# Zeros ahead of the first products, a broadcast in float32r halves, and a clamp on GpSimd: one change to an attention and two-MLP kernel

## The chip, the core and the metric

The kernel runs on one core of a Trainium2 chip. The metric is the device time of one execution in microseconds (us), the median over the runs of a kernel. A core has five engines that run side by side, each through its own instructions in order: TensorE (PE in the profile, with its weight loads as PEld), VectorE (DVE), ScalarE (ACT), GpSimd (POOL) and SyncE (SP), which here issues all DMA transfers. They wait for each other through semaphores.

## What is computed

Two batches of eight heads, 576 positions, head size 64: causal attention with a bias from a running sum, then an MLP with a leaky ReLU, then a second MLP with four experts that are weighted by probabilities.

```
scores = q @ k^T / 8
cum    = cumsum(max(s, 0))                      # per head, along the sequence
scores = where(causal mask, -1e9, scores + min(-(cum_i - cum_j), 0))
x      = softmax(scores) @ v                    # heads side by side: 1152 x 512
x      = leaky(x @ w_in) @ w_out                # 512 -> 2048 -> 512, float64 inputs
p      = probs / (sum(probs) + 1e-9)
out    = sum over e of p[:, e] * (relu(x @ w1[e]) @ w2[e])   # 4 experts, 512 -> 1024 -> 512
```

`moe_w_in` and `moe_w_out` come as float64; the kernel sees them as pairs of 32-bit words.

## The kernel before, in words

Everything of the MLPs is multiplied as float32r in two halves (a high part and the remainder): `products` (L150) issues three matmuls for each pair, high by high, low by high, high by low. The attention is plain float32, which TensorE runs in two passes for each product.

**Attention.** The 1152 rows are cut into four parts, each for four pairs of heads; one part and one pair make a `Unit` (L319). For each of its tiles of 128 queries and each head of the pair it runs four steps, which trail each other by a few tiles: `scores` (L329) masks the diagonal block of `nck` on GpSimd (L339), multiplies q by k (L342, tile `ps_sc`), lets VectorE combine the product with `nck` and take the row minimum (L343, tile `z`), and ScalarE take the exponential (L347); `transposes` (L349, tile `ps_pt`) turns z for the product with v, `values` (L359, tile `ps_o`) multiplies and scales by the row sums (L367, L368, L371), and `finish` (L373, tile `ps_x`) turns the result into the halves of x (L387, L388).

**The running sum.** `cumulative` (L274) loads s for all 16 heads, 16 partitions of 576, and scans it on VectorE (L281, tile `cum`). `nck` is its row for each of two heads, spread over all 128 partitions. For the first unit `load_pair` does this by a float32 product of a column of the identity with `cum` (L308, tile `ps_nck`) and a copy by ScalarE (L309); for all others cum goes to DRAM (L282) and comes back by a DMA with a stride of zero (L312).

**Weights.** `load_w` brings pieces of 128x1024. A piece of w_in or w_out is converted from float64 once (`convert`, L73, 16 pieces in all): two loads fill `r64` (a pool of two buffers, in which `pos` and `cum` also lie), ScalarE scales the upper words (L84), VectorE clamps (L85), shifts (L86), and joins the lower word and the sign (L87, L88). The result goes to DRAM (L97) for the later phases. Every piece is then split: ScalarE rounds it to the high half (L104), GpSimd subtracts (L105).

**Order.** The program is written as generators that are woven together (`weave`, L413): attention of the first part, then the first MLP on 512 rows beside the attention of the next, and so on. The order in which instructions finally stand on each engine is set by the framework's scheduler at build time, which has its own cost estimates, so that an edit in one place moves instructions in others. `ps_sc` and the pool of `ps_pt`, `ps_x` and `ps_nck` have two PSUM buffers each.

The quoted lines are the clamp and what stands around it, as printed in the functions below.

Of the kernel before, what the change touches and what calls it, by code (L numbers as in the profile page):

```python
# [8 lines left out]
F32 = mybir.dt.float32  # L9
# [3 lines left out]
ALU = mybir.AluOpType  # L13
# [5 lines left out]
def attention_moe_moe2(ctx: ExitStack, tc: tile.TileContext, q, k, v, s, w_in, w_out, probs, w1, w2, out):  # L19
# [31 lines left out]
    def f32(ap):  # L51
        return ap.bitcast(F32)
# [20 lines left out]
    def convert(src, raw, rows):  # L73

        r64 = r64p.tile([P, 1024, 2], U32, tag="r64", name="r64")
        for i in range(2):
            a, c = slice(i * rows // 2, (i + 1) * rows // 2), slice(i * 512, (i + 1) * 512)  # L80
            nc.sync.dma_start(r64[:, c].rearrange("p (a b) t -> p a (b t)", a=rows // 2), src[:, a])
        lower, upper = r64[:, :, 0], r64[:, :, 1]
        bits = raw.bitcast(U32)
        nc.scalar.activation(raw, upper.bitcast(F32), AF.Abs, scale=65536.0)  # L84
        nc.vector.tensor_scalar(raw, raw, 2.0, LARGEST, ALU.max, ALU.min)  # L85
        nc.vector.tensor_scalar(bits, bits, 3, None, ALU.logical_shift_left)  # L86
        nc.vector.scalar_tensor_tensor(bits, lower, 29, bits, ALU.logical_shift_right, ALU.bitwise_or)  # L87
        nc.vector.scalar_tensor_tensor(bits, upper, 0x80000000, bits, ALU.bitwise_and, ALU.bitwise_or)  # L88
# [205 lines left out]
    def load_pair(n, b, hp, i0, i1):  # L294


        q0, q1 = tiles[i0][0], tiles[i1 - 1][2]
        rows, h = slice(hp * P, (hp + 1) * P), b * H + 2 * hp
        kr = ap.tile([P, S], F32, tag="kr", name="kr")
        nc.sync.dma_start(kr[:, :q1], k[b].rearrange("h d s -> (h d) s")[rows, :q1])  # L300
        qz, vs = q_pads[n % 2], v_s[n % 4]
        for j in range(2):
            nc.sync.dma_start(qz[j * D : (j + 1) * D, j, : q1 - q0], q[b, 2 * hp + j, :, q0:q1])
        nck = ap.tile([P, 2, S], F32, tag="nck", name="nck")
        if n == 0:
            for j in range(2):
                ps = ps_t.tile([P, 512], F32, tag="pt", name="ps_nck")[:, :q1]
                nc.tensor.matmul(ps, ident[:BH, h + j : h + j + 1].to_broadcast([BH, P]), cum[:, :q1], start=True, stop=True)  # L308
                nc.scalar.copy(nck[:, j, :q1], ps)  # L309
        else:  # L310
            src = cum_d[h : h + 2, 0:q1]
            nc.sync.dma_start(nck[:, :, :q1], bass.AP(tensor=src.tensor, offset=src.offset, ap=[[0, P], [S, 2], [1, q1]]))  # L312
        full = min(q1 // P, QT - 1)
        nc.sync.dma_start(vs[:, :full].rearrange("p t h c -> p t (h c)"), v[b, : full * P, rows].rearrange("(t p) c -> p t c", p=P))
        if i1 == QT:
            nc.sync.dma_start(vs[P - S % P :, QT - 1].rearrange("p h c -> p (h c)"), v[b, full * P :, rows])
        return kr, qz, nck, vs
# [178 lines left out]
```

## Time and profile before

| | |
|---|---|
| median of 3 runs | 768.6 us (768.29 to 769.13) |
| the profiled execution: its own time | 767.84 us |
| its span, first to last instruction | 766.1 us |
| TensorE busy | 746.2 us, 97% of the span |
| VectorE, ScalarE, GpSimd busy | 317.7, 287.9, 229.6 us |
| moved by DMA | 79.56 MB |

All rows shown here come from that one execution. Times in them count from the span's start. A row of the timeline gives the start, the length, the engine, the line in the kernel, the operation, what is written from what, and in brackets how long the engine had been idle before and what ended that. TensorE's products overlap their neighbours, so their lengths add up to more than the time that they take together. Names of tiles appear without their buffer numbers (`raw`, `z`), and a DMA's issue on SP is not its landing.

### The profile page before, as it was taken

Reading aid. Unit: us, or ns where it says so; the run is one execution under the profiler, and the core shown is the slowest. Engines: PE = TensorE matmul, PEld = TensorE weight load, DVE = VectorE, ACT = ScalarE, POOL = GpSimd, SP = SyncE. Lnnn points to the kernel's source line nnn. Section 1 sums busy time; section 2 is a strip of 40 time slices with the busy share of each in tenths; the row PEclk is TensorE's granted clock in tenths of the full one; section 3 lists DMA queues with packets and bytes.
Section 4 is the critical chain, followed back from the end, with each engine's and each line's share of the span. In section 5 each row is a group of like instructions: output and inputs, shape, how many; then the busy total and the mean of one; then the engine's idle time right before and its main releaser. Section 6 shows DMA issues by size and latency. Waiting matters only on the chain.

```text
span 766.1 us, 10681 instructions
## 1 busy us (share of the span) xinstructions
PE 746.2 (97%) x4124; PEld 648.6 (85%) x4124; DVE 317.7 (41%) x663; ACT 287.9 (38%) x587; POOL 229.6 (30%) x174
## 2 busy tenths in 40 slices
PE   7798999999999999999999999999999999999997
PEld 4576788778889999999898888988989889888886
DVE  3998685974544443323322222222222222222222
ACT  3766665564565564654320221211303112032010
POOL 3551143453344244676311220312203121122100
PEclk9899999999999999999999999999999999999999
DMA  8778945764243222435210110202001101000002
GB/s 254 245 229 279 316 147 178 258 210 151 66 142 115 79 83 83 154 129 163 78 56 28 56 54 1 83 28 56 29 28 56 56 30 53 28 28 0 1 28 96
DMA packets 44931, 79.56 MB, mean 104 GB/s; under 512 B 4528, under 2 KB 23472, under 8 KB 44880
## 3 DMA queue, kind: packets, MB, share of 16 engines
q1 hardware_dynamic: 44880, 78.88, 31.5%
q8 instruction: 32, 0.52, 0.3%
q14 instruction: 19, 0.16, 0.1%
HBM read 68.08 MB, written 10.78 MB: 103 GB/s over the span
## 4 chain that ended last, share of the span: by engine, by line
PE 87%; DVE 5%; DMA 5%; issue 1%; POOL 0%; ACT 0%; SPq 0%; POOLq 0%; DVEq 0%; ACTq 0%
PE ps_d L154 39%; PE ps_u L154 37%; PE ps_sc L342 5%; PE ps_o L365 4%; PE ps_pt L356 2%; DMA r<-in_moe_w_in_dram 1%; DMA kr<-in_k_dram 1%; DVE z L343 1%; DVE raw L87 1%; DMA r<-in_moe_w_out_dram 1%; DMA pn<-in_moe_domain_probs_dram 1%; DMA nck<-cum_d 1%; DVE raw L88 1%; DVE st L367 0%; DVE raw L86 0%
## 5 line engine op out<-in xcount | busy, mean ns | idle before, releaser
L105 POOL TENSOR_TENSOR w<-raw,w 128x1024 fp32r<-128x1024 f32 x80 | 193.9, 2434 | 376.4 <-ACT w L104 374.9
L154 PE MATMUL ps_u<-y,w 128*128 128x320 f32 (+1 forms) x1152 | 201.5, 336 | 0.7 <-DVE yacc L207 0.7
L154 PEld LDWEIGHTS ps_u<-y,w 128*128 128x128 f32 x1152 | 185.1, 188 | 17.0 <-ACT w L104 0.9
L154 PE MATMUL ps_d<-w,ht 128*128 128x512 f32 x864 | 197.3, 389 | 0.0
L154 PEld LDWEIGHTS ps_d<-w,ht 128*128 128x128 f32 x864 | 161.8, 188 | 33.2
L104 ACT CAST w<-raw 128x1024 fp32r<-128x1024 f32 x80 | 83.1, 1044 | 170.7 <-issue 163.1
L154 PE MATMUL ps_u<-x,w 128*128 128x320 f32 (+1 forms) x576 | 116.7, 349 | 1.5 <-DVE ht L188 1.0
L154 PE MATMUL ps_d<-ht,w 128*128 128x320 f32 (+1 forms) x576 | 116.9, 349 | 0.0
L191 DVE SCALAR_TENSOR_TENSOR ht<-ps_u,ht 128x320 fp32r<-128x320 f32 (+1 forms) x96 | 53.6, 558 | 146.9 <-ACT ht L190 146.9
L154 PEld LDWEIGHTS ps_u<-x,w 128*128 128x128 f32 x576 | 92.0, 189 | 11.3 <-issue 2.3
L190 ACT ACTIVATE ht<-ps_u 128x320 fp32r<-128x320 f32 (+1 forms) x96 | 47.1, 491 | 142.0 <-PE ps_u L154 142.0
L154 PEld LDWEIGHTS ps_d<-ht,w 128*128 128x128 f32 x576 | 91.4, 188 | 8.7 <-issue 1.3
L228 DVE SCALAR_TENSOR_TENSOR oacc<-ps_d,pn,oacc 128x512 f32<-128x512 f32 x63 | 47.3, 751 | 122.8 <-PE ps_d L154 122.8
L342 PE MATMUL ps_sc<-kr,qz 128*128 128x448 f32 (+4 forms) x192 | 68.7, 455 | 4.5 <-DVE mn L343 4.3
L339 POOL TENSOR_SCALAR_AFFINE_SELECT nck<-nck 128x128 f32<-128x128 f32 x80 | 33.2, 428 | 120.7 <-DVE mn L343 60.0
L365 PEld LDWEIGHTS ps_o<-vs,pv 128*128 128x128 f32 x480 | 63.1, 196 | 6.0 <-DVE xo L371 1.9
L365 PE MATMUL ps_o<-vs,pv 128*128 128x64 f32 x480 | 64.0, 271 | 1.3 <-DVE xo L371 1.0
L347 ACT ACTIVATE z<-z,mn 128x512 f32<-128x512 f32 (+4 forms) x80 | 48.4, 606 | 44.2 <-DVE mn L343 43.8
L343 DVE CUSTOM_DVE_ANT_0 z<-ps_sc,nck 128x512 f32<-128x512 f32 (+4 forms) x80 | 40.7, 511 | 32.9 <-PE ps_sc L342 23.6
L357 ACT COPY pv<-ps_pt 128x512 f32<-128x512 f32 (+3 forms) x96 | 39.1, 422 | 25.1 <-PE ps_pt L356 22.9
L342 PEld LDWEIGHTS ps_sc<-kr,qz 128*128 128x128 f32 x192 | 32.9, 197 | 15.7 <-DVE mn L343 7.2
L356 PE MATMUL ps_pt<-ident,z 128*128 128x128 f32 x240 | 42.1, 279 | 3.5 <-ACT pv L357 2.4
(43 smaller groups left out, 354.1 us busy)
## 6 DMA issues: line engine op xcount, KB each, us to landing
raw<-w_f SPq DMA_DIRECT2D x32, 512.0 KB, 3.2
raw<-in_moe_w_dram SPq DMA_DIRECT2D x32, 512.0 KB, 3.4
r<-in_moe_w_in_dram SPq DMA_DIRECT2D x16, 512.0 KB, 6.5
w_f<-raw SPq DMA_DIRECT2D x16, 512.0 KB, 3.3
r<-in_moe_w_out_dram SPq DMA_DIRECT2D x16, 512.0 KB, 5.6
nck<-cum_d SPq DMA_DIRECT2D x8, 576.0 KB, 5.9
vs<-in_v_dram SPq DMA_DIRECT2D x12, 256.0 KB, 4.6
kr<-in_k_dram SPq DMA_DIRECT2D x8, 288.0 KB, 4.9
```

The source lines that it names most:

```text
L104: nc.scalar.copy(w[:, 0], raw)
L105: nc.gpsimd.tensor_tensor(w[:, 1], raw, f32(w[:, 0]), ALU.subtract)
L154: nc.tensor.matmul(ps, a, b, start=(i == 0), stop=(i == len(pairs) - 1))
L190: nc.scalar.activation(hi, ps, AF.Relu)
L191: nc.vector.scalar_tensor_tensor(lo, ps, 0.0, f32(hi), ALU.max, ALU.subtract)
L228: nc.vector.scalar_tensor_tensor(oacc[tt], ps, p, oacc[tt], ALU.mult, ALU.add)
L342: nc.tensor.matmul(ps, self.qz[:, j, own], self.kr[:, keys], start=True, stop=True)
L343: nc.vector.tensor_tensor_reduce(out=z[:, keys], in0=ps, in1=nck[:, j, keys], scale=-(D ** -0.5), scalar=3.0e38 if pc == 0 else mn[:, 0:1] ...
L347: nc.scalar.activation(z, z, AF.Exp, bias=mn[:, pc : pc + 1], scale=-1.0, accum_out=self.st[i][:, j : j + 1])
L356: nc.tensor.transpose(pt[:, (kt - k0) * P : (kt - k0 + 1) * P], z[:, tiles[kt][0] : tiles[kt][2]], ident)
L357: nc.scalar.copy(pv[:, k0:k1].rearrange("p t q -> p (t q)"), pt)
L365: nc.tensor.matmul(o[:, j], pv[:, kt], self.vs[:, kt, j], start=(kt == 0), stop=(kt == i))
```

## The change

Three edits. First, 8 products of a 128x128 tile of zeros by itself are issued on TensorE at the start, into a PSUM tile that nothing reads. Second, the first unit's `nck` is no longer a float32 product: the first 512 columns of `cum` are split into a high half (ScalarE) and a remainder (VectorE) in a new tile `cum0`, the two columns of the identity are copied as float32r (`pick`), and each head's row is two accumulated float32r products. `cum0` is a third allocation in the pool of two `r64` buffers. Third, the clamp in `convert` runs on GpSimd instead of VectorE. Below the edits, line numbers grow by up to 12.

```diff
@@ convert
         nc.scalar.activation(raw, upper.bitcast(F32), AF.Abs, scale=65536.0)
-        nc.vector.tensor_scalar(raw, raw, 2.0, LARGEST, ALU.max, ALU.min)
+        nc.gpsimd.tensor_scalar(raw, raw, 2.0, LARGEST, ALU.max, ALU.min)
         nc.vector.tensor_scalar(bits, bits, 3, None, ALU.logical_shift_left)
@@ cumulative
-    cum = None
+    cum0 = None
+    pick = const.tile([BH, 2], F32R, name="pick")
...
+        idle = ap.tile([P, P], F32, tag="idle", name="idle", bufs=1)
+        nc.vector.memset(idle, 0.0)
+        nothing = ps_t.tile([P, 512], F32, tag="pt", name="nothing")
+        for _ in range(8):
+            nc.tensor.matmul(nothing[:, :P], idle, idle, start=True, stop=True)
         pos, cum = (r64p.tile([P, 2048], F32, tag="r64", name=n)[:BH] for n in ("pos", "cum"))
+        nc.scalar.copy(pick, ident[:BH, :2])
...
         nc.vector.tensor_tensor_scan(cum, spos, zero, 0.0, ALU.add, ALU.add)
+        cum0 = r64p.tile([P, 2048], F32R, tag="r64", name="cum0")[:BH, : 2 * sizes[0]].rearrange("p (l k) -> p l k", l=2)
+        nc.scalar.copy(cum0[:, 0], cum[:, : sizes[0]])
+        nc.vector.tensor_tensor(cum0[:, 1], cum[:, : sizes[0]], f32(cum0[:, 0]), ALU.subtract)
         nc.sync.dma_start(cum_d, cum)
@@ load_pair, first unit
-                nc.tensor.matmul(ps, ident[:BH, h + j : h + j + 1].to_broadcast([BH, P]), cum[:, :q1], start=True, stop=True)
+                for l in range(2):
+                    nc.tensor.matmul(ps, pick[:, j : j + 1].to_broadcast([BH, P]), cum0[:, l, :q1], start=(l == 0), stop=(l == 1))
```

The scheduler gives the whole early part another order. Three places, with the program's instructions as they stand on an engine.

TensorE from its first instruction on, before (`ps_nck` is the broadcast, `ps_sc` the scores, `ps_pt` the transposes):

```order
0 L491 UNCONDITIONAL_BRANCH
1 L308 MATMUL ps_nck<-cum,ident 128x512 x2
2 L342 MATMUL ps_sc<-kr,qz 128x512 x2
3 L342 MATMUL ps_sc<-kr,qz 128x384
4 L356 MATMUL ps_pt<-ident,z 128x128 x4
```

and with the change:

```order
0 L503 UNCONDITIONAL_BRANCH
1 L282 MATMUL nothing<-idle 128x128 x8
2 L354 MATMUL ps_sc<-kr,qz 128x512
3 L320 MATMUL ps_nck<-cum_135,pick 128x512
4 L354 MATMUL ps_sc<-kr,qz 128x512
5 L320 MATMUL ps_nck<-cum_135,pick 128x512 x3
6 L354 MATMUL ps_sc<-kr,qz 128x384 x2
```

The zeros stand first, and the first scores ahead of the broadcast, which is now four products of one pass.

GpSimd behind its first memsets, before (L339 is the mask, L105 the subtraction for the split weights):

```order
12 L339 AFFINE_SELECT nck<-nck 128x128 x13
13 L105 TENSOR_TENSOR w<-raw,w 128x1024
14 L339 AFFINE_SELECT nck<-nck 128x128 x4
15 L105 TENSOR_TENSOR w<-raw,w 128x1024
16 L339 AFFINE_SELECT nck<-nck 128x128 x4
```

and with the change:

```order
12 L351 AFFINE_SELECT nck<-nck 128x128 x10
13 L85 TENSOR_SCALAR raw<-raw 128x1024
14 L351 AFFINE_SELECT nck<-nck 128x128
15 L85 TENSOR_SCALAR raw<-raw 128x1024
16 L351 AFFINE_SELECT nck<-nck 128x128 x4
17 L105 TENSOR_TENSOR w<-raw,w 128x1024
18 L351 AFFINE_SELECT nck<-nck 128x128 x3
19 L105 TENSOR_TENSOR w<-raw,w 128x1024
20 L85 TENSOR_SCALAR raw<-raw 128x1024
21 L351 AFFINE_SELECT nck<-nck 128x128 x2
```

The clamps stand between masks, the first two of them ahead of the first subtraction. Among the first masks, five of the first unit now stand ahead of the second unit's; before it was two.

VectorE where the second piece of weights is converted, before (z operations are L343, those named mn end them; `pn` and `prow` are the probabilities):

```order
41 L343 ISA z,mn<-ps_sc,nck 128x384
42 L343 ISA mn 128x1
43 L66 RECIPROCAL prow<-prow 128x9
44 L368 RECIPROCAL st<-st 128x2
45 L87 SCALAR_TENSOR_TENSOR raw<-r_556,raw 128x1024
46 L371 TENSOR_TENSOR xo<-ps_o,st 128x128
47 L67 TENSOR_TENSOR pn<-pn,prow 128x36
48 L367 TENSOR_SCALAR st<-st 128x2
49 L88 SCALAR_TENSOR_TENSOR raw<-r_556,raw 128x1024
50 L368 RECIPROCAL st<-st 128x2
51 L343 ISA z,mn<-ps_sc,nck 128x384
```

and with the change, from the probabilities on (L355 is L343, r_564 the first piece; L379 and L380 are L367 and L368, L383 is L371):

```order
37 L67 TENSOR_TENSOR pn<-pn,prow 128x36
38 L355 ISA z,mn<-ps_sc,nck 128x512
39 L355 ISA mn 128x1
40 L86 TENSOR_SCALAR raw<-raw 128x1024
41 L355 ISA z,mn<-ps_sc,nck 128x384
42 L355 ISA mn 128x1
43 L87 SCALAR_TENSOR_TENSOR raw<-r_564,raw 128x1024
44 L383 TENSOR_TENSOR xo<-ps_o,st 128x128
45 L379 TENSOR_SCALAR st<-st 128x2
46 L88 SCALAR_TENSOR_TENSOR raw<-r_564,raw 128x1024
47 L380 RECIPROCAL st<-st 128x2
48 L383 TENSOR_TENSOR xo<-ps_o,st 128x128
```

L67 now stands ahead of the whole first conversion, and z operations stand between the steps of a conversion; the clamp is gone from this queue. On SP the load of the second unit's `nck` stands behind three loads of v instead of ahead of them.

## Rows read from the trace of the kernel before

**Rows 1.** The page: busy us of each engine with its share of the span and its instructions, and the chain that ended last, by engine.

```profile
PE 746.2 (97%) x4124; PEld 648.6 (85%) x4124; DVE 317.7 (41%) x663; ACT 287.9 (38%) x587; POOL 229.6 (30%) x174
...
PE 87%; DVE 5%; DMA 5%; issue 1%; POOL 0%; ACT 0%; SPq 0%; POOLq 0%; DVEq 0%; ACTq 0%
```

**Rows 2.** Three stretches: us, then busy us and instructions of PE, PEld, DVE, ACT and POOL, the granted clock as a share of full speed, DMA's busy share and GB/s.

```profile
20.00:40.00 20.00, 16.62 (x86) 12.43 (x87) 18.37 (x49) 13.10 (x35) 9.76 (x10) 0.85 0.78 247
40.00:60.00 20.00, 18.80 (x114) 14.56 (x113) 18.53 (x43) 13.73 (x34) 10.04 (x10) 0.97 0.74 239
...
160.00:766.00 606.00, 601.48 (x3345) 535.58 (x3343) 196.47 (x382) 190.96 (x366) 167.86 (x93) 1.00 0.21 68
```

**Rows 3.** Waits of TensorE from 13 to 140 us: who waited for whom, us in total, times, the longest.

```profile
PE ps_sc L342 <- DVE mn L343: 4.3, 7, 2.2
PE ps_pt L356 <- ACT pv L357: 2.4, 4, 1.2
PE ps_o L365 <- DVE xo L371: 1.0, 2, 0.8
```

**Rows 4.** The timeline from 0 to 15 us, some rows of it, by engine.

```profile
1.66 1.19 SPq L303 DMA_DIRECT2D qz<-in_q_dram  x2
...
7.08 1.57 SPq L314 DMA_DIRECT2D vs<-in_v_dram  x3
...
3.01 1.35 DVE L281 TENSOR_TENSOR_SCAN cum<-pos 16x576 f32<-16x576 f32 x1
...
10.42 0.69 DVE L343 CUSTOM_DVE_ANT_0 z<-ps_sc,nck 128x512 f32<-128x512 f32 x1 [6.06 <-PE ps_sc L342]
...
13.39 0.56 DVE L343 CUSTOM_DVE_ANT_0 z<-ps_sc,nck 128x384 f32<-128x384 f32 x1 [0.58 <-POOL nck L339]
...
7.23 0.29 POOL L339 TENSOR_SCALAR_AFFINE_SELECT nck<-nck 128x128 f32<-128x128 f32 x1 [3.06 <-ACT nck L309]
...
12.51 1.03 POOL L339 TENSOR_SCALAR_AFFINE_SELECT nck<-nck 128x128 f32<-128x128 f32 x4 [3.27 <-DMA nck<-cum_d]
...
4.50 3.75 PE L308 MATMUL ps_nck<-cum,ident 16*128 16x512 f32 x4 [4.50 <-DVE cum L281]
8.18 5.06 PE L342 MATMUL ps_sc<-kr,qz 128*128 128x512 f32 x6
13.03 0.94 PE L356 MATMUL ps_pt<-ident,z 128*128 128x128 f32 x4
...
14.46 0.60 PE L356 MATMUL ps_pt<-ident,z 128*128 128x128 f32 x4
```

**Rows 5.** Groups by line and shape on ScalarE and VectorE from 0 to 180 us: count, busy us, mean ns of one, idle time before them.

```profile
L387 ACT CAST x<-ps_x 128x512 fp32r<-128x512 f32 x4 | 2.3, 568 | 0.0
...
L388 DVE TENSOR_TENSOR x<-ps_x,x 128x512 fp32r<-128x512 f32 x4 | 2.7, 679 | 0.0
```

**Rows 6.** DMA issues from 0 to 14 us: KB of one, median us from issue to landing.

```profile
qz<-in_q_dram SPq DMA_DIRECT2D x4, 128.0 KB, 3.2
```

**Rows 7.** Groups by line and shape on VectorE from 0 to 180 us, columns as in rows 5; and the line on the instructions of L367 over the whole span, with the shortest, median and longest in ns.

```profile
L87 DVE SCALAR_TENSOR_TENSOR raw<-r,raw 128x1024 uint32<-128x1024 uint32 x16 | 23.3, 1454 | 0.1
L88 DVE SCALAR_TENSOR_TENSOR raw<-r,raw 128x1024 uint32<-128x1024 uint32 x16 | 21.0, 1310 | 0.0
L367 DVE TENSOR_SCALAR st<-st 128x2 f32<-128x2 f32 x28 | 16.0, 572 | 3.4 <-ACT z L347 3.3
L86 DVE TENSOR_SCALAR raw<-raw 128x1024 uint32<-128x1024 uint32 x16 | 12.8, 798 | 0.1
L85 DVE TENSOR_SCALAR raw<-raw 128x1024 f32<-128x1024 f32 x16 | 11.0, 688 | 13.9 <-ACT raw L84 13.9
...
L367 DVE TENSOR_SCALAR st<-st x35: 142/170/2371, 13.9 to 245.5; 128x2 f32<-128x2 f32 x35
...
  ACT raw L84: 13.9, 10
```

(The last line is of L85's instructions: until what their engine sat idle before them, us and times.)

**Rows 8.** Groups by line and shape on GpSimd from 0 to 180 us, columns as in rows 5.

```profile
L105 POOL TENSOR_TENSOR w<-raw,w 128x1024 fp32r<-128x1024 f32 x15 | 37.7, 2518 | 17.1 <-ACT w L104 17.1
L339 POOL TENSOR_SCALAR_AFFINE_SELECT nck<-nck 128x128 f32<-128x128 f32 x58 | 26.9, 479 | 86.3 <-DMA nck<-cum_d 40.4 <-DVE mn L343 39.5 <-ACT nck L309 4.5
L290 POOL MEMSET qz<- 64x512 f32 x4 | 2.1, 519 | 0.1
L292 POOL MEMSET vs<- 64x128 f32 x4 | 0.6, 196 | 0.0
```

**Rows 9.** The timeline from 27 to 47 us, some rows of it, by engine; and the stretch from 0 to 80 us for the instructions of L85 alone, columns as in rows 2.

```profile
27.52 3.32 POOL L105 TENSOR_TENSOR w<-raw,w 128x1024 fp32r<-128x1024 f32 x1
...
28.75 2.14 DVE L67 TENSOR_TENSOR pn<-pn,prow 128x36 f32<-128x36 f32 x1
...
31.02 1.21 DVE L88 SCALAR_TENSOR_TENSOR raw<-r,raw 128x1024 uint32<-128x1024 uint32 x1
...
44.97 2.47 DVE L86 TENSOR_SCALAR raw<-raw 128x1024 uint32<-128x1024 uint32 x1
...
32.82 0.92 PE L342 MATMUL ps_sc<-kr,qz 128*128 128x256 f32 x4 [2.23 <-DVE mn L343]
...
0.00:80.00 80.00, 5.49 (x8) 0.96 0.81 254
```

**Rows 10.** The stretch from 34 to 42 us, columns as in rows 2; the last but two is the granted clock.

```profile
34.00:42.00 8.00, 8.00 (x34) 6.59 (x33) 6.83 (x16) 5.07 (x14) 2.06 (x2) 0.57 0.82 250
```

More of the change, by code (lines that the diff above doesn't have):

```diff
@@ L271, in attention_moe_moe2 @@
     cum_d = dram.tile([BH, S], F32, name="cum_d")
-    cum = None
+    cum0 = None
+    pick = const.tile([BH, 2], F32R, name="pick")
     def cumulative():
-        nonlocal cum
+        nonlocal cum0
+        idle = ap.tile([P, P], F32, tag="idle", name="idle", bufs=1)
[3 more added lines that the diff above has]
+            nc.tensor.matmul(nothing[:, :P], idle, idle, start=True, stop=True)
         pos, cum = (r64p.tile([P, 2048], F32, tag="r64", name=n)[:BH] for n in ("pos", "cum"))
+        nc.scalar.copy(pick, ident[:BH, :2])
         spos, zero, cum = pos[:, :S], pos[:, S : 2 * S], cum[:, :S]
```

## The prediction

> **What bounds the kernel now.** I read the page's busy shares and chain first [rows 1]. TensorE is busy 97% of the span and holds 87% of the chain that ended last, so the run ends when its products are done: only its idle time, its time at the low clock, or products that disappear can move the end. The stages say where such time lies [rows 2]: of 606 us behind 160, TensorE misses 4.5; from 20 to 60 it misses 4.6 of 40, and there VectorE is busy 18.4 and 18.5 of every 20. All three edits act ahead of 160 us. TensorE's longest waits between 13 and 140 us [rows 3]: 4.3 + 1.0 us end with VectorE, 2.4 with an eviction by ScalarE. So VectorE is the engine to relieve, early. The execution read here took 767.84 us for a span of 766.1; the median of the runs is 768.6, 0.76 higher. A measurement of this kernel tells about 0.2% (1.5 us) from no change.
>
> **Zeros and the first broadcast.** The first products start at 4.50, when the scan (3.01 + 1.35) is done [rows 4]. Four passes of ps_nck hold TensorE until 8.18; then come the scores, and on VectorE the first z starts at 10.42 and the third at 13.39. The clock is low all this while: four transposes take 0.94 us at 13.03 but 0.60 at 14.46, and a pass of 512 columns some 0.85 us (3.7 by 4) where it should take half.
>
> Added: one memset on VectorE, which waits there for the scan's input, and 8 products of 128 columns in two passes each. At the low clock a pass of that size takes some 0.21 us (0.94 less the last one's tail, by four), so 16 take 3.4 us, from about 1.2 to 4.6. TensorE had no work then, so they cost nothing. Added behind the scan: a cast on ScalarE and a subtraction on VectorE of 512 columns, 0.57 and 0.68 by the x rows of the same width [rows 5]; the low half is there at 4.36 + 0.6 + 0.7 + hops = 5.8. TensorE no longer waits for it with everything: the first scores now stand ahead. They wait for kr and qz; the latter's two issues begin at 1.66 and end at 2.85, and such a load lands 3.2 us behind its issue [rows 4, 6], say 5.5. Then follow two scores and four float32r passes instead of four float32 ones.
> - Clock still low: scores 1.7, ps_nck 0.43, scores 1.7, three ps_nck 1.3, so 5.5 + 5.1 = 10.6; the first nck is complete at 10.2, and eviction (0.6), mask (0.29) and hops put z at 11.3, the third (its scores wait for the buffer that the first z frees) at 13.5. Nothing gained against 13.39.
> - Clock high from the first scores on: half of all that, the first z at 9.0, the third at 10.5: 2.9 us gained.
>
> Before, products ran from 4.50 on and the clock was up only near 13.5; the zeros start 3.3 us sooner, so I expect it up sooner, but not at once. I take **1.0**, a third of the way, ends 0 and 2.9. On SP the load of the second unit's nck goes behind three vs issues, 1.57 us later [rows 4]; the mask that waited for it at 12.51 held the masks of the first unit behind it, and in the new order five of these stand ahead, so I cost the move at nothing. If that cover fails, it is those 1.57 us.
>
> **The clamp.** VectorE loses 16 x 688 ns = 11.0 us [rows 7]. GpSimd gets 16 clamps of 128x1024, which no row prices. Below: a memset grows from 196 ns at 128 columns to 519 at 512, 0.84 ns a column, so 0.95 us at 1024. Above: the subtraction of two inputs, 2.4 us [rows 8, 9]. The nearest row is the mask, also one input and a scalar operation: 0.29 us at 128 columns [rows 4], less some 0.09 that the memsets show as fixed, 1.56 ns a column, 1.7 us. I take **1.6**.
>
> GpSimd's work isn't free to VectorE. At 27.52 a subtraction of 3.32 us runs; VectorE's 36-column product L67, issued at 28.75, is done only at 30.89, when the subtraction ends; at 44.97 L86 takes 2.47 where 0.69 is usual, until another subtraction ends [rows 9]. [...]
>
> How much it is: undisturbed, L367 takes 0.17 (its median), L86 0.69 like L85, L87 and L88 1.21 (the row at 31.02). Over 0 to 180 us the stretched time on VectorE is L367 16.0 - 28 x 0.17 = 11.2, L86 12.8 - 16 x 0.69 = 1.8, L87 23.3 - 16 x 1.21 = 3.9, L88 21.0 - 16 x 1.21 = 1.6, L67 some 2.0: 20.5 us, for GpSimd work of 37.7 + 58 x 0.29 = 54.5 net and 64.6 as recorded [rows 7 to 9]. So one us on GpSimd costs VectorE 0.32 to 0.38. Clamps of 25.6 us cost 8.8: net relief 11.0 - 8.8 = 2.2 us. At 0.95 us it is 5.8, at 2.4 it is -2.0. Eight of the 16 clamps start before 80 us [rows 9]; behind that TensorE misses little [rows 2]. Half of the relief reaches the end: **1.1**, ends -1.0 and 2.9.
>
> **The order of the early rows.** The one large hole of TensorE is 30.6 to 32.82, 2.23 us [rows 9]; the z that it needs stood behind L67 and L88. [...] In the new order L67 stands ahead of the first subtraction and can meet a clamp at most; but the second L86 now stands where the first subtraction runs. So I expect a hole again, shorter by 2.1 - 1.2 = **0.9** (L67's delay against a clamp's remainder), and the clock to fall once as before. Ends: 0, and 2.2 + 3.4 = 5.6 if neither comes back. The float32r passes also save some 1 us of TensorE's work at the high clock, but they stand in the first 11 us, which are counted above.
>
> Sum: 767.84 - 1.0 - 1.1 - 0.9 = 764.8; with the 0.76 of the median, **765.6 us**.
>
> **Rivals.**
> - Everything goes through: clock up at once, no hole, cheap clamp: 2.9 + 2.9 + 5.6 = 11.4 us, median 757.2. For it: all four terms are in the rows. Against: 37.7 us of subtractions still meet VectorE [rows 8], so holes should come again. A half way to it, 760, is likelier than the whole.
> - [...] Before, VectorE sat idle at L85 for the ScalarE step 10 times, 13.9 us [rows 7]: conversions arrive late. If VectorE now comes to L86 before the clamp is done, each late conversion costs 1.6 + 0.1 (hop) - 0.69 = 1.0 us more, and masks for the next z queue behind a clamp that itself waits for the load. At five of the eight early ones that is 5.0, less the 1.0 at the front, and without the gain in the order: 771.8 us, median 772.6. With a clamp of 2.4 us the five cost 9.0, median 776.6. It decides when fewer than about 1.7 us of other VectorE work stand between the load's arrival and L86; for it, GpSimd's queue has two clamps in a row around one mask; against it, the new order has whole z operations ahead of each L86 and the probabilities moved ahead too. [...]
> [...]
>
> **Numbers.** The forecast (faster by 1.6 to 7) 0.45, the large gain (over 7) 0.13, no change 0.17, slower 0.25 (of it 0.05 beyond 772). Faster 0.58, same 0.17, slower 0.25. The likeliest case alone is 762 to 767; as cases of both signs count, the range goes from 758.5, between the half and the whole of the first rival, to 772.0, just short of the second one's price at five conversions.
>
> **What would show it.** Front: products named nothing from about 1.2 to 4.6 us; z at 9.0 to 11.3, and a pass of scores near 0.43 us apart instead of 0.85. Clamp: L85 on GpSimd at 1.0 to 2.4 us; VectorE's busy time to 160 us lower by 2 rather than 11, with L367 or L86 stretched beyond before. Order: a hole of TensorE near 30 us shorter than 2.2, with one stretch of clock at half behind it. Wrong if VectorE idles before L86 for GpSimd as long as it did at L85 for ScalarE, if masks wait behind clamps and z behind masks, or if TensorE falls to the low clock more than once behind 15 us.

## The result and the profile after

The change made the kernel slower: 777.12 us, the median of 4 runs (774.25 to 778.44), against 768.44 for the kernel before in the same session. The ratio is 1.0113, 95% interval 1.0095 to 1.0132. The forecast was 765.6 us in 758.5 to 772.0. The profiled execution took 777.59 us for a span of 775.4.

Busy time and the chain, from the page of the changed kernel (columns as in [rows 1]):

```profile
PE 747.4 (96%) x4140; PEld 651.7 (84%) x4140; DVE 316.6 (41%) x649; ACT 288.5 (37%) x589; POOL 292.4 (38%) x190
...
PE 81%; DMA 8%; DVE 5%; issue 2%; POOL 2%; SPq 1%; ACT 1%; POOLq 0%; ACTq 0%
```

VectorE's busy time hardly moved, 317.7 to 316.6, though 11 us of clamps left it; GpSimd has 62.8 more. Where TensorE lost the time is read from the same stretches as in [rows 2], with the first 180 us as a fourth:

```profile
20.00:40.00 20.00, 15.78 (x103) 12.23 (x102) 16.46 (x41) 12.56 (x32) 16.67 (x13) 1.00 0.70 210
40.00:60.00 20.00, 16.33 (x100) 12.73 (x101) 16.59 (x39) 13.62 (x35) 18.61 (x13) 1.00 0.78 247
160.00:766.00 606.00, 601.50 (x3333) 535.06 (x3334) 202.05 (x384) 193.61 (x370) 179.23 (x97) 0.99 0.22 71
...
0.00:180.00 180.00, 156.58 (x852) 125.21 (x853) 128.06 (x281) 105.44 (x243) 128.06 (x101) 0.96 0.69 221
```

From 40 to 60 us TensorE was busy 18.80 before and 16.33 now. GpSimd went from 10.04 to 18.61 of 20. That stretch is not the price, though: a kernel among the experiments below (e1), faster than both, is busy 16.07 there. Most of the loss stands from 100 to 180 us, before and then with the change:

```profile
100.00:140.00 40.00, 39.02 (x220) 33.15 (x219) 29.85 (x55) 23.54 (x51) 17.97 (x13) 1.00 0.59 196
140.00:180.00 40.00, 38.88 (x200) 32.06 (x199) 31.45 (x67) 21.48 (x52) 15.72 (x13) 1.00 0.66 222
...
100.00:140.00 40.00, 36.53 (x202) 30.23 (x200) 26.46 (x49) 22.39 (x48) 32.23 (x18) 1.00 0.60 196
140.00:180.00 40.00, 35.00 (x165) 28.26 (x166) 31.33 (x50) 20.75 (x49) 30.61 (x17) 0.91 0.62 203
```

TensorE missed 2.1 of these 80 us before and misses 8.5 now, and the clock granted at 0.91 over the last 40 us costs up to another 3.6 (40 x 0.09). The waits of TensorE from 13 to 140 us, as in [rows 3]:

```profile
PE ps_o L377 <- DVE xo L383: 5.9, 4, 2.2
PE ps_sc L354 <- DVE mn L355: 4.0, 5, 1.2
PE ps_sc L354 <- DMA kr<-in_k_dram: 1.8, 1, 1.8
PE ps_pt L368 <- ACT pv L369: 0.9, 2, 0.5
```

Most of them end with VectorE still, 9.9 us now against 5.3. The two longest come at the end of this window and behind it: 2.82 us until 140.29, for an eviction by ScalarE (L369), and 3.40 until 169.73, for VectorE's `ht` (L188). VectorE's groups to 180 us (columns as in [rows 7]), then GpSimd's (as in [rows 8]), then L85's instructions (shortest, median, longest in ns) and who waited for them:

```profile
L87 DVE SCALAR_TENSOR_TENSOR raw<-r,raw 128x1024 uint32<-128x1024 uint32 x16 | 31.4, 1965 | 0.1
L88 DVE SCALAR_TENSOR_TENSOR raw<-r,raw 128x1024 uint32<-128x1024 uint32 x16 | 25.3, 1580 | 0.1
L86 DVE TENSOR_SCALAR raw<-raw 128x1024 uint32<-128x1024 uint32 x16 | 13.8, 862 | 16.8 <-POOL raw L85 13.5 <-DMA vs<-in_v_dram 3.2
L379 DVE TENSOR_SCALAR st<-st 128x2 f32<-128x2 f32 x26 | 10.4, 400 | 8.0 <-ACT z L359 7.7
...
L85 POOL TENSOR_SCALAR raw<-raw 128x1024 f32<-128x1024 f32 x16 | 59.1, 3692 | 27.4 <-ACT raw L84 27.4
L105 POOL TENSOR_TENSOR w<-raw,w 128x1024 fp32r<-128x1024 f32 x14 | 36.1, 2587 | 2.6 <-ACT w L104 1.6 <-DMA qz<-in_q_dram 1.0
...
L85 POOL TENSOR_SCALAR raw<-raw x16: 3618/3625/4578, 19.0 to 170.7; 128x1024 f32<-128x1024 f32 x16
...
  DVE raw L86: 13.5, 9
```

A clamp takes 3.62 us on GpSimd, against 0.69 on VectorE. VectorE stood idle for it nine times, 13.5 us. And the subtractions L105 waited 1.6 us for ScalarE's rounding where it was 17.1 [rows 8]: they now come late on their own account. The front, as in [rows 4]:

```profile
1.04 3.78 PE L282 MATMUL nothing<-idle 128*128 128x128 f32 x16 [1.04 <-DVE idle L279]
4.97 1.50 PE L354 MATMUL ps_sc<-kr,qz 128*128 128x512 f32 x2
6.40 0.49 PE L320 MATMUL ps_nck<-cum,pick 16*128 16x512 f32 x1
6.82 1.13 PE L354 MATMUL ps_sc<-kr,qz 128*128 128x512 f32 x2
9.62 0.69 DVE L355 CUSTOM_DVE_ANT_0 z<-ps_sc,nck 128x512 f32<-128x512 f32 x1 [3.91 <-POOL nck L351]
11.43 0.56 DVE L355 CUSTOM_DVE_ANT_0 z<-ps_sc,nck 128x384 f32<-128x384 f32 x1 [0.51 <-POOL nck L351]
```

The first z stands at 9.62 (before 10.42) and the third at 11.43 (before 13.39). No hole stands near 30 us; one of 2.19 us now ends at 24.32, where TensorE waits for `xo` (L383). First L67, as in [rows 9], then the clock from 34 to 42, as in [rows 10]:

```profile
24.18 0.18 DVE L67 TENSOR_TENSOR pn<-pn,prow 128x36 f32<-128x36 f32 x1
...
34.00:42.00 8.00, 7.51 (x45) 5.48 (x45) 6.12 (x20) 5.72 (x16) 5.72 (x3) 1.00 0.88 293
```

So the first z came sooner, L67 ran undisturbed, and the clamp cost more than both gave.

### The profile page after: what moved, and what is told of

Its sections match the earlier page's. It is cut to its first block, busy times and chain, and to the rows that moved or that the text cites. A ratio compares the mean times of both kernels' runs of the same rounds, so it can differ in the third digit from the quotient of the medians.

```text
span 775.4 us, 10738 instructions
## 1 busy us (share of the span) xinstructions
PE 747.4 (96%) x4140; PEld 651.7 (84%) x4140; DVE 316.6 (41%) x649; ACT 288.5 (37%) x589; POOL 292.4 (38%) x190
## 4 chain that ended last, share of the span: by engine, by line
PE 81%; DMA 8%; DVE 5%; issue 2%; POOL 2%; SPq 1%; ACT 1%; POOLq 0%; ACTq 0%
PE ps_d L154 37%; PE ps_u L154 35%; PE ps_o L377 4%; PE ps_sc L354 3%; DMA r<-in_moe_w_in_dram 3%; PE ps_pt L368 2%; DVE raw L87 2%; DMA vs<-in_v_dram 1%; POOL raw L85 1%; DVE raw L88 1%; DMA nck<-cum_d 1%; DMA pn<-in_moe_domain_probs_dram 1%; DMA r<-in_moe_w_out_dram 1%; DVE raw L86 1%; DVE st L379 0%
## 5 line engine op out<-in xcount | busy, mean ns | idle before, releaser
L105 POOL TENSOR_TENSOR w<-raw,w 128x1024 fp32r<-128x1024 f32 x80 | 194.3, 2439 | 361.2 <-ACT w L104 358.6
L154 PE MATMUL ps_u<-x,w 128*128 128x320 f32 (+1 forms) x576 | 120.7, 355 | 3.4 <-DVE ht L188 3.4
L154 PE MATMUL ps_d<-ht,w 128*128 128x320 f32 (+1 forms) x576 | 114.4, 347 | 0.0
L354 PE MATMUL ps_sc<-kr,qz 128*128 128x448 f32 (+4 forms) x192 | 66.7, 444 | 7.5 <-DVE mn L355 5.5
L85 POOL TENSOR_SCALAR raw<-raw 128x1024 f32<-128x1024 f32 x16 | 59.1, 3692 | 27.4 <-ACT raw L84 27.4
L351 POOL TENSOR_SCALAR_AFFINE_SELECT nck<-nck 128x128 f32<-128x128 f32 x80 | 37.1, 482 | 54.9 <-DVE mn L355 25.2
L355 DVE CUSTOM_DVE_ANT_0 z<-ps_sc,nck 128x512 f32<-128x512 f32 (+4 forms) x80 | 40.3, 512 | 29.5 <-PE ps_sc L354 18.7
L369 ACT COPY pv<-ps_pt 128x512 f32<-128x512 f32 (+3 forms) x96 | 38.6, 423 | 26.6 <-PE ps_pt L368 25.5
```

Source lines behind the costliest of these rows:

```text
L85: nc.gpsimd.tensor_scalar(raw, raw, 2.0, LARGEST, ALU.max, ALU.min)
L105: nc.gpsimd.tensor_tensor(w[:, 1], raw, f32(w[:, 0]), ALU.subtract)
L154: nc.tensor.matmul(ps, a, b, start=(i == 0), stop=(i == len(pairs) - 1))
L354: nc.tensor.matmul(ps, self.qz[:, j, own], self.kr[:, keys], start=True, stop=True)
L355: nc.vector.tensor_tensor_reduce(out=z[:, keys], in0=ps, in1=nck[:, j, keys], scale=-(D ** -0.5), scalar=3.0e38 if pc == 0 else mn[:, 0:1] ...
L369: nc.scalar.copy(pv[:, k0:k1].rearrange("p t q -> p (t q)"), pt)
```

## The experiments

Ratios are against the kernel before in the same session (medians 767.3 to 768.9 us), with 95% intervals. A thousandth is 0.77 us. GpSimd's busy time is that of the first 180 us in the profiled run, 67.5 in the kernel before.

| kernel | median us | ratio | GpSimd us |
|---|---|---|---|
| the change | 777.12 | 1.0113 (1.0095 to 1.0132) | 128.1 |
| e1: clamp back on VectorE | 763.18 | 0.9935 (0.9910 to 0.9960) | 74.1 |
| e2: clamp alone | 778.44 | 1.0128 (1.0102 to 1.0154) | 125.0 |
| e3: zeros alone | 764.29 | 0.9972 (0.9947 to 0.9996) | 69.2 |
| e4: broadcast alone | 767.56 | 0.9991 (0.9976 to 1.0006) | 67.7 |
| e5: half a clamp | 776.64 | 1.0120 (1.0096 to 1.0143) | 101.0 |
| e6: one operation of two | 774.16 | 1.0075 (1.0055 to 1.0095) | 119.0 |
| e7: spare clamps beside e1 | 775.65 | 1.0096 (1.0078 to 1.0114) | 129.7 |
| e8: three copies in e1 | 766.65 | 0.9990 (0.9974 to 1.0007) | 65.4 |
| e9: 32 columns | 762.17 | 0.9928 (0.9905 to 0.9950) | 81.8 |
| e10: clamps of a ready tile beside e1 | 785.66 | 1.0236 (1.0216 to 1.0257) | 121.9 |
| e11: 64 memsets beside e1 | 771.26 | 1.0042 (1.0023 to 1.0062) | 128.8 |
| e12: the change without masks | 771.26 | 1.0047 (1.0032 to 1.0062) | 102.3 |
| e13: e1 without masks | 757.36 | 0.9865 (0.9850 to 0.9880) | 44.9 |
| e14: a quarter clamp | 768.98 | 1.0027 (1.0007 to 1.0047) | 87.6 |
| e15: e1, clamp twice | 769.42 | 1.0011 (0.9992 to 1.0031) | 69.8 |
| e16: e8 and e15 together | 768.31 | 0.9995 (0.9977 to 1.0013) | 65.2 |
| e17: e12, subtractions on ScalarE | 757.55 | 0.9868 (0.9842 to 0.9894) | 62.4 |
| e18: e13, subtractions on ScalarE | 760.40 | 0.9887 (0.9841 to 0.9932) | 3.4 |

**Which part.** e1 takes one line of the change back; e2, e3 and e4 keep one edit of the three each.

```diff
-        nc.gpsimd.tensor_scalar(raw, raw, 2.0, LARGEST, ALU.max, ALU.min)
+        nc.vector.tensor_scalar(raw, raw, 2.0, LARGEST, ALU.max, ALU.min)
```

> The change with its clamp put back on VectorE; zeros and float32r broadcast stay. Theory A (the clamp did it: 3.62 us each on GpSimd where VectorE took 0.69, in the chain of every conversion): the loss of 8.7 us goes, and what is left is the front alone, with the third z near 11.4 us as in the changed kernel against 13.39 before; 765.5 to 768.5 us. Theory B (the new order of the early part did it, by zeros and broadcast as much as by the clamp): still 772 us or more.

For e2, against the change (e3 has e1's line and takes back the broadcast alone; e4 has e1's line and takes back the zeros alone):

```diff
-        for _ in range(8):
-            nc.tensor.matmul(nothing[:, :P], idle, idle, start=True, stop=True)
...
-                for l in range(2):
-                    nc.tensor.matmul(ps, pick[:, j : j + 1].to_broadcast([BH, P]), cum0[:, l, :q1], start=(l == 0), stop=(l == 1))
+                nc.tensor.matmul(ps, ident[:BH, h + j : h + j + 1].to_broadcast([BH, P]), cum[:, :q1], start=True, stop=True)
```

> The kernel before with only the clamp moved to GpSimd. Theory A: 16 clamps of 3.62 us, slower by 7 to 11 us, 776 to 779 us, with VectorE idle before L86 for some 13 us in all. Theory B: under 771 us.

> The kernel before with only the products of zeros. If the zeros raise the clock sooner (theory A's front): the float32 broadcast stays at the low clock or nearly, the scores behind it run in half the time, the third z comes by 1 to 2 us sooner than 13.39; 766.5 to 768.4 us. If what comes sooner at the front is lost again before TensorE is full (theory B): 768 to 769 us or, by a worse order, more.

> The kernel before with only the float32r broadcast from halves. Four passes of 512 columns at the low clock take 1.7 us instead of 3.4, less the wait for the low half (some 1.4 us behind the scan): the third z 0 to 1 us sooner than 13.39; 767 to 769 us by theory A. Theory B: the order decides, anything from 765 to 773 us.

The clamp alone costs as much as the whole change, within the intervals; zeros and broadcast with the clamp on VectorE are faster than both kernels by their intervals (e1, 0.9935). The clamp's price is the difference of the change and e1: 0.0178, 13.7 us. The zeros alone give 2.1 us and the broadcast alone nothing that its interval tells from zero. The medians of e1 and e3 lie below what I had expected of them. In e4 (no zeros) two passes of scores of 512 columns take 2.05 us at 4.88 and the first z comes at 11.82; in e1 the same two take 1.80 at 4.87 and the z comes at 9.82. The third z, in e1 and then in e3:

```profile
12.38 0.56 DVE L355 CUSTOM_DVE_ANT_0 z<-ps_sc,nck 128x384 f32<-128x384 f32 x1 [1.25 <-PE ps_sc L354]
...
14.49 0.55 DVE L348 CUSTOM_DVE_ANT_0 z<-ps_sc,nck 128x384 f32<-128x384 f32 x1
```

In e1 it comes 1.0 us sooner than before, in e3 1.1 later, and both are faster than the kernel before. So that z does not tell the gain, and the runs do not show where all of it comes from. Where the clamp's price is paid shows from 100 to 180 us in e1:

```profile
100.00:140.00 40.00, 40.00 (x221) 34.00 (x220) 33.37 (x59) 25.81 (x55) 17.70 (x14) 1.00 0.72 236
140.00:180.00 40.00, 40.00 (x211) 33.60 (x210) 28.26 (x62) 20.82 (x49) 17.14 (x18) 1.00 0.57 185
```

e1 misses nothing there, at full clock. The changed kernel's 8.5 + 3.6 = 12.1 us at most are the larger part of the 14.7 by which the two profiled spans differ (775.4 and 760.7).

**How the price grows.** Three versions of the change with less on GpSimd (in e14 256 columns, in e9 32):

```diff
-        nc.gpsimd.tensor_scalar(raw, raw, 2.0, LARGEST, ALU.max, ALU.min)
+        nc.gpsimd.tensor_scalar(raw[:, :512], raw[:, :512], 2.0, LARGEST, ALU.max, ALU.min)
+        nc.vector.tensor_scalar(raw[:, 512:], raw[:, 512:], 2.0, LARGEST, ALU.max, ALU.min)
```

> The change with the clamp cut in two: GpSimd takes columns 0 to 511, VectorE columns 512 to 1023. If the price of the clamp on GpSimd sets the loss (3.62 us against 0.69), half a clamp should take some 1.85 us there and 0.35 on VectorE and lose about half: 763.2 (clamp on VectorE) + 13.9 x (1.85 - 0.69)/(3.62 - 0.69) = 769, that is 767 to 771 us. If any clamp in GpSimd's queue, whatever its length, is what hurts (two engines that wait for each other, masks behind it): 774 us or more.

> The changed kernel with 256 of 1024 columns clamped on GpSimd (estimated 1.2 to 1.3 us each, between 0.64 measured for 32 columns and 2.06 for 512) and the rest on VectorE. 32 columns: 762.2 us, 512: 776.6, 1024: 777.1. If the loss grows with the time up to half a clamp: 767 to 771. If it sets in at a point (a mask or a join just misses its slot): 762 to 765 or 774 to 777.

> The changed kernel, but the clamp is cut: GpSimd takes 32 of the 1024 columns, VectorE the other 992. GpSimd's instruction keeps its place in the queue (still behind ScalarE's step and ahead of VectorE's shift, with masks behind it) but should take some 0.2 us instead of 3.62. The half clamp (2.1 us each) had cost as much as the whole one, so its length alone does not tell what is paid for. Time theory (masks and VectorE pay for the microseconds that GpSimd works): back to that of the kernel with the clamp on VectorE, 762 to 766 us. Wait theory (GpSimd stands at the head of its queue waiting for ScalarE, 24 to 27 us in all, with masks behind it; and one more hop lies in each conversion): 771 to 777, as the half clamp. The order that the scheduler makes with a clamp in GpSimd's queue, if it alone were bad: also 771 to 777.

and e6, against the change, with the maximum alone (the upper limit is left out):

```diff
-        nc.gpsimd.tensor_scalar(raw, raw, 2.0, LARGEST, ALU.max, ALU.min)
+        nc.gpsimd.tensor_scalar(raw, raw, 2.0, None, ALU.max)
```

> The change with the upper bound of the clamp left out (GpSimd takes the maximum alone). If GpSimd's price goes by the number of operations, the instruction takes about 1.9 us and the time is near 769 us by the same line as the half clamp; if it goes by columns and operands alone, it stays at 3.6 us and 777 us.

Medians of one clamp: 0.74 us for 32 columns (at the least 0.32), 1.37 for 256, 2.12 for 512, 2.77 for one operation, 3.62 for the whole. Against e1 they cost -0.5, 7.1, 14.2, 10.8 and 13.7 us. My straight line failed at the half, which costs as much as the whole, and one operation took neither of the two lengths that I had named for it. The sliver (e9) matters most: with 32 columns the clamp keeps its place in GpSimd's queue and its wait for ScalarE (18.1 us idle before it), and costs nothing. So neither the hop to another engine nor the place alone is the price; it takes GpSimd's time.

**Time of whose?** Against e1, e7 keeps the clamp on VectorE and adds one that nobody waits for; e10 adds it on a constant tile that is always ready (its definition is not shown); e11 adds four memsets of such a tile instead:

```diff
             nc.sync.dma_start(w_f32[unit], raw)
+            spare = ap.tile([P, 1024], F32, tag="spare", name="spare", bufs=1)
+            nc.gpsimd.tensor_scalar(spare, raw, 2.0, LARGEST, ALU.max, ALU.min)
```

```diff
             nc.sync.dma_start(w_f32[unit], raw)
+            nc.gpsimd.tensor_scalar(spare, spare, 2.0, LARGEST, ALU.max, ALU.min)
```

```diff
             nc.sync.dma_start(w_f32[unit], raw)
+            for _ in range(4):
+                nc.gpsimd.memset(spare, 2.0)
```

> Zeros and broadcast as in the change, clamp on VectorE, and for each of the 16 conversions one more clamp on GpSimd that reads the finished piece and writes a tile that nobody reads: the same 59 us of GpSimd, but outside the chain of the conversion. Theory A1 (the loss is the longer chain of each conversion, VectorE idle before L86): 763 to 766 us. [...]

> Clamp on VectorE; beside it GpSimd does 16 clamps of 128x1024 of a constant tile by itself, one for each conversion. They wait for nothing and nobody waits for them; only GpSimd's time is used, 16 x 3.6 us. Time theory: 771 to 777 us, as with 16 spare clamps that waited for the finished piece (775.65). Wait theory: 763 to 767, since GpSimd never stands waiting with masks behind it. Part of a difference can come from their place: without a wait they may stand earlier in the queue, nearer to the first masks.

> Clamp on VectorE; beside it 64 memsets of 128x1024 on GpSimd into a tile that nothing reads, four for each conversion, estimated 0.95 us each (196 ns at 128 columns, 519 at 512), so as much GpSimd time as 16 clamps, without reading SBUF and in shorter pieces. [...] If masks pay because they stand in GpSimd's queue: 769 to 775 (shorter pieces, so a mask waits less than behind a clamp of 3.6 us), VectorE's joins not stretched.

e8, e15 and e16 put on e1 what the clamp does to the conversion, without GpSimd: a longer chain (three copies by ScalarE of 1.05 us), more of VectorE's time (the clamp twice, at its line in the diff below), and both:

```diff
         nc.scalar.activation(raw, upper.bitcast(F32), AF.Abs, scale=65536.0)
+        for _ in range(3):
+            nc.scalar.copy(raw, raw)
         nc.vector.tensor_scalar(raw, raw, 2.0, LARGEST, ALU.max, ALU.min)
+        nc.vector.tensor_scalar(raw, raw, 2.0, LARGEST, ALU.max, ALU.min)
```

> Zeros and broadcast as in the change, clamp on VectorE, and three copies in place on ScalarE ahead of each clamp, about 3.1 us: the chain of each conversion is as much longer as with the clamp on GpSimd (2.9 us), but GpSimd has no more work than before. Theory A1: 772 to 778 us. [...]

> The kernel with the clamp on VectorE (763.2 us), and there the clamp is done twice: 16 more instructions of 688 ns, 11 us more for VectorE ahead of 180 us, in the conversions, nothing more for GpSimd. If VectorE's time there is what TensorE ends up paying for, about one for one: 771 to 776. If VectorE has slack enough and the loss came another way (GpSimd's subtractions for the split, the order): 762 to 766.

> Clamp on VectorE, done twice, and three copies in place by ScalarE in each conversion: the longer chain and the lost VectorE time together, nothing more for GpSimd. If the costs add: 763.2 + 4.2 + 5.8 = 773. If a later piece and a busier VectorE make each other worse: 775 to 778, and nothing is left of the 13.7 to explain. If they cover each other: 767 to 770, and a third way on GpSimd's side has the rest.

Spare clamps cost 12.4 us more than e1, ready ones 23.1 (they stand earlier, the last at 93.8 us), memsets 8.2. The copies cost 4.2, the second clamp 5.8, both together 4.6, less than the sum of the two. Neither e8 nor e16 is clean: in both the last two conversions end behind 180 us (14 of 16 ahead of it). What these show is that work of GpSimd that nobody waits for can cost as much as the clamp, and that a conversion later by 3 us costs a third of it.

They lose it in another place, though. From 20 to 100 us TensorE misses 12.2 us in e7, 15.5 in e10 and 10.4 in e11 (9.0 in e1). The clock granted in the four stretches of 20 us is 1.00, 0.83, 0.74, 1.00 in e7, 0.57, 0.78, 0.71, 1.00 in e10 and 0.72, 0.94, 0.83, 1.00 in e11, against 1.00, 1.00, 0.95, 0.97 in e1. From 100 to 180 they miss 2.5, none and 0.8 us, where the change misses 8.5. So they do not show by which way the clamp costs its time.

**What the clamp meets on GpSimd.** There are two pairs, each to be read by itself. e12 and e13 leave the masks of the diagonal blocks out, e17 and e18 the subtractions too (ScalarE writes a copy instead, so that products are other ones):

```diff
-            nc.gpsimd.affine_select(nck[:, j, a:kw], nck[:, j, a:kw], [[-1, P]], ALU.is_ge, MASKED, 0, 1)
```

```diff
-        nc.gpsimd.tensor_tensor(w[:, 1], raw, f32(w[:, 0]), ALU.subtract)
+        nc.scalar.copy(w[:, 1], raw)
```

> The changed kernel without the masks of the diagonal blocks (GpSimd's affine_select left out, so queries see later keys); GpSimd keeps clamps and subtractions. To be read against the next kernel alone (also without masks, clamp on VectorE), not against the kernel before. Masks theory (z waits for masks that queue behind clamps): the two differ by under 4 us. VectorE theory (joins, shifts and small products stretched beside GpSimd's clamps, and the wait for the clamp itself): this one is 9 to 16 us longer, as with masks.

> Zeros and new broadcast, clamp on VectorE, without the masks. Both theories: some 758 to 763 us, since with masks it took 763 and the masks cost TensorE a few us of waits at most (z waited 4.2 us for masks there).

> The changed kernel without masks, and with the low half of each split weight written by a ScalarE copy in place of GpSimd's subtraction (so the products are not those of the reference, and ScalarE has 80 x 1.05 us more). GpSimd does clamps alone behind its first memsets. To be read against the next kernel alone. Subtractions as the third way: under 6 us above it (the longer chain, VectorE's wait). VectorE theory (clamps stretch VectorE's instructions and hold the head of its queue): 9 to 16 us above it, as with masks and subtractions.

> The same without masks and with ScalarE's copy for the subtraction, but the clamp on VectorE: GpSimd does nothing behind its first memsets. Some 755 to 765 us by either theory; VectorE's L85 to L88 should show their undisturbed lengths here (0.69, 0.69, 1.21, 1.21 us) if GpSimd's instructions are what stretches them.

Without masks the clamp costs 0.0182, 14.0 us (plus or minus 1.6): as much as with them, so the masks that queue behind clamps are not the way. The place is the same too: from 100 to 180 us e12 misses 7.3 us and e13 none. Without subtractions it costs -0.0019, -1.5 us (plus or minus 4.0): nothing. That also refutes my "VectorE theory" as written for e17: the clamps alone, with the wait for them, do no harm. VectorE's groups to 180 us in e17, columns as above:

```profile
L88 DVE SCALAR_TENSOR_TENSOR raw<-r,raw 128x1024 uint32<-128x1024 uint32 x16 | 20.1, 1257 | 0.1
L87 DVE SCALAR_TENSOR_TENSOR raw<-r,raw 128x1024 uint32<-128x1024 uint32 x16 | 19.5, 1221 | 0.2
L86 DVE TENSOR_SCALAR raw<-raw 128x1024 uint32<-128x1024 uint32 x16 | 11.0, 689 | 12.2 <-POOL raw L85 12.2
L378 DVE TENSOR_SCALAR st<-st 128x2 f32<-128x2 f32 x28 | 5.4, 194 | 9.9 <-ACT z L358 9.8
```

and the same four in e12, where the subtractions are there:

```profile
L87 DVE SCALAR_TENSOR_TENSOR raw<-r,raw 128x1024 uint32<-128x1024 uint32 x16 | 29.4, 1840 | 0.4 <-DVE mn L354 0.2
L88 DVE SCALAR_TENSOR_TENSOR raw<-r,raw 128x1024 uint32<-128x1024 uint32 x16 | 21.7, 1358 | 0.0
L86 DVE TENSOR_SCALAR raw<-raw 128x1024 uint32<-128x1024 uint32 x16 | 20.7, 1292 | 12.8 <-POOL raw L85 12.7
L378 DVE TENSOR_SCALAR st<-st 128x2 f32<-128x2 f32 x27 | 15.0, 555 | 12.8 <-ACT z L358 12.7
```

VectorE waits as long for the clamp in both (12.2, 12.7 us). What differs is the stretched time. With GpSimd idle (e18) the four take 1.215, 1.219, 0.688 and 0.164 us. Over these lengths e12 loses 10.0 + 2.2 + 9.7 + 10.6 = 32.5 us; e13, with the clamp on VectorE and two subtractions more, loses 15.3 by the same count (its L85 among them); e17 loses 1.5. So in this pair the clamp on GpSimd doubles what VectorE loses. How, the timeline of e12 shows:

```profile
115.50 3.73 POOL L85 TENSOR_SCALAR raw<-raw 128x1024 f32<-128x1024 f32 x1 [3.08 <-ACT raw L84]
...
119.20 5.18 POOL L105 TENSOR_TENSOR w<-raw,w 128x1024 fp32r<-128x1024 f32 x2
119.27 2.86 DVE L86 TENSOR_SCALAR raw<-raw 128x1024 uint32<-128x1024 uint32 x1 [2.71 <-POOL raw L85]
122.04 2.37 DVE L378 TENSOR_SCALAR st<-st 128x2 f32<-128x2 f32 x1
...
127.70 0.44 PE L367 MATMUL ps_pt<-ident,z 128*128 128x128 f32 x2 [2.74 <-DVE x L399]
```

The end of the clamp lets two things start: L86 on VectorE, which waited for it, and the two subtractions that queued behind it on GpSimd. They start 0.07 us apart and collide: L86 takes 2.86 us instead of 0.69, and an addition on two columns (L378) 2.37 instead of 0.16. The two joins and the `x` (L399) stand behind them on VectorE, and TensorE waits 2.74 us for that x. The changed kernel has the same picture:

```profile
159.04 3.63 POOL L85 TENSOR_SCALAR raw<-raw 128x1024 f32<-128x1024 f32 x1
162.64 5.14 POOL L105 TENSOR_TENSOR w<-raw,w 128x1024 fp32r<-128x1024 f32 x2
162.70 2.86 DVE L86 TENSOR_SCALAR raw<-raw 128x1024 uint32<-128x1024 uint32 x1 [1.93 <-POOL raw L85]
165.60 3.26 DVE L87 SCALAR_TENSOR_TENSOR raw<-r,raw 128x1024 uint32<-128x1024 uint32 x1
168.78 0.28 DVE L355 CUSTOM_DVE_ANT_0 z<-ps_sc,nck 128x128 f32<-128x128 f32 x1
169.73 0.80 PE L154 MATMUL ps_u<-x,w 128*128 128x512 f32 x1 [3.40 <-DVE ht L188]
```

VectorE does nothing but two conversion steps from 162.70 to 168.86, a z and the `ht` (L188) stand behind them, and TensorE waits 3.40 us. Behind that wait the clock falls: it is granted at 0.68 from 170 to 180 us.

**What stays open.** Shown, within the plus or minus 4.0 us of the second pair: with the subtractions in GpSimd's queue the clamp costs 14 us, without them nothing. That the subtractions come late is not the price by itself: in e12 they waited 19.3 us for ScalarE's rounding, much as in the kernel before, and the clamp cost as much; and of the waits that the trace lists for TensorE to 180 us, in e12 and in the changed kernel, none ends with a subtraction. Read from rows, not isolated: that the 14 us come through these collisions. The wait of 2.82 us until 140.29 is a step further off: ScalarE stood 2.84 us at L84 for a conversion's load, with the eviction behind it. VectorE's stretched time rises by 10.2 us from e1 (16.5) to the change (26.7), its waits for L85 or for the step ahead by 6.8, and 11.0 us of clamps leave it, 6 us net. The stretched time does not set the price by itself: by the same count it is some 35 us in e11, which costs 8.2, and some 26 in e10, which costs 23.1. Not settled is why the clamp costs 13.7 when 11 us more in e15 cost 5.8. My guess is that the scheduler knew of e15's work and ordered around it, while a collision comes unplanned in front of whatever stands behind it; no run held the order fixed. e17 and e18 also free VectorE of every stretch by subtractions, so the clamp may have cost nothing there because VectorE had time to spare; no run keeps these two apart.

## Why the prediction was wrong, point by point

**The front: inside its ends, by a measure that does not carry.** I took 1.0 us in ends of 0 to 2.9; the third z came 2.0 us sooner. Zeros ran from 1.04 to 4.8 as laid out. The second scores were already short: their two passes took 1.13 us where those of the first took 1.50, so sooner than the third of the way that I granted. The low clock at the front I had read from lengths alone: in the kernel before, passes of 512 columns took 1.10 us on the mean up to 14 us, 1.06 from 34 to 41, where the granted clock was low [rows 10], and 0.62 from 42 to 140; but at the front the granted clock reads 1.00, from 0 to 20 us. In e1, front and order together gave 5.0 us where I had 1.0 + 0.9, with the third z only 1.0 sooner; 2.1 of it is time that TensorE no longer misses from 100 to 180 us. I had counted the gain by the third z, and e3 gains with a later one.

**The clamp's price: wrong, and outside both bounds.** This is the step that failed: its term was 1.1 us gained, ends -1.0 and 2.9, and against e1 the clamp on GpSimd loses 13.7. I priced one clamp 1.6 us from the mask's slope, ends 0.95 and 2.4; it took 3.62. The upper bound failed because I held that an instruction with two inputs costs more than one with a single input: the subtraction takes 2.40, the clamp with one operation 2.77, with two 3.62.

**The stretch factor: wrong in kind.** I charged VectorE 0.35 us for each microsecond of GpSimd, whatever it did. In e17, 59 us of clamps stretched VectorE by 1.5; in e12, with subtractions, it was 32.5. So the kind of work counts, and the clamp decides when the subtraction runs. What stretched in the changed kernel were the joins (L87 1965 ns, before 1454), not the small additions that I had named (L379 400 ns, before 572). The end at 2.4 us was also off in the sum: the formula gives -2.2, not -2.0. With the true price my own formula would have said 11.0 - 59.1 x 0.35 = -9.7, half of it at the end: 4.8 us slower than without the clamp, against 13.7 measured. So the better price alone would not have saved the number. Which way the rest goes is open in part, as said above.

**Relief reaching the end by half:** e15 agrees, 5.8 of 11.0 us. What came was no relief.

**The order: right for L67, not for the whole.** L67 took 0.18 and no low clock followed in 34 to 42. But VectorE waited 2.65 us for the load of the probabilities (L64, at 23.07) with `xo` behind it in its queue, and so TensorE's hole of 2.19 us came sooner instead of shrinking. I had costed the loss of cover elsewhere at nothing: granted 0.94 from 60 to 80, 0.89 from 80 to 100, 0.91 from 140 to 180. That the clock falls more than once behind 15 us was one of my signs of being wrong, and it came. No run shows the 3.4 us in my upper end of 5.6 as time lost: they are an estimate, the 0.43 of full speed that was not granted over the 8 us of [rows 10], and the changed kernel was granted 1.00 over the same 8 us.

**The rival.** The slower rival named 776.6 for a dear clamp and gave the sign that would show it, VectorE idle before L86 for GpSimd: 13.5 us, nine times, as before at L85 for ScalarE (13.9, ten times). Its number and sign came true, its reason only in part. The longer chain that it stood on costs 4.2 us in e8, and nothing that its interval tells from zero in e17, where GpSimd has no subtractions. I gave it 0.25, and 0.05 beyond 772; with the bound on the clamp drawn wider upward, its dear form would have had more.

## What to carry to other kernels

These rows suggest what to ask. Before moving an elementwise step to an idle engine, ask what stands in that engine's queue behind it, and whether the end of the moved step releases that work and the next step of its own chain at once, on engines whose instructions lengthen each other (L86 here from 0.69 to 2.86 us). Busy share says nothing on that: GpSimd stood at 30%, and 16 instructions of 3.6 us cost 14 us. Where no row prices an operation on an engine, rows of other operations give no upper bound, and the forecast should carry the dear case with a real chance.

## What the hardware showed

VectorE's instructions were not lengthened over all the 3.62 us of a clamp of 128x1024. In e7, one spare clamp with VectorE's instructions beside it:

```profile
59.58 3.62 POOL L99 TENSOR_SCALAR spare<-raw 128x1024 f32<-128x1024 f32 x1
...
60.09 1.07 DVE L86 TENSOR_SCALAR raw<-raw 128x1024 uint32<-128x1024 uint32 x1
61.20 1.23 DVE L87 SCALAR_TENSOR_TENSOR raw<-r,raw 128x1024 uint32<-128x1024 uint32 x1
62.34 0.88 DVE L381 TENSOR_SCALAR st<-st 128x2 f32<-128x2 f32 x1
62.46 1.23 DVE L88 SCALAR_TENSOR_TENSOR raw<-r,raw 128x1024 uint32<-128x1024 uint32 x1
```

L86 begins 0.51 us behind the clamp's start and takes 1.07, done 1.58 behind: 0.89 and its own 0.69. L87 begins 1.62 behind and takes 1.23, in e18 1.215. L381, of 0.16 us, begins 2.76 behind and takes 0.88, done 3.64 behind: 3.48 and its own length; the join L88, begun 0.12 later, takes 1.23. Both times recur. In e7 (clamp at 27.22) an L87 begun 0.39 behind takes 1.72, done 2.11 behind, 0.90 and 1.21; in e17 (134.29) an L378 begun 0.44 behind takes 0.63, done 1.07 behind, 0.91 and 0.16. In e10 (63.59) the clamp on VectorE begins 2.76 behind and takes 1.41, done 4.17 behind, 3.48 and 0.69; in e17 (143.66) an L378 begun 3.36 behind takes 0.29, done 3.65 behind, 3.48 and 0.17. No run here shows the cause.

A memset of 128x1024 took 0.95 us on GpSimd where it stands alone in e11 (1.02 on the mean of 64), as estimated from its smaller ones. Behind sixteen passes of zeros the products were short sooner: in the change the two passes of scores that start at 6.82 took 1.13 us, while in e4, without zeros, the two at 8.01 still took 2.08. The granted clock does not tell the two apart: it reads 1.00 from 0 to 10 us in both. In e1, with the same zeros, 0.67 was granted from 10 to 20 us, after TensorE was busy 1.04 of the 2 us to 10; in the change TensorE was busy 0.82 of them, and 1.00 was granted.
